# Top-k attention followed by an exact-GELU MLP: eleven odd items turned by VectorE and DRAM, with their product a slot later

## The chip, the cores and the metric

The kernel runs on one core of a Trainium2 chip. The metric is the device time of one execution in microseconds; the time before is the median of three runs. The engines are named as the profile names them: PE is TensorE (PEld its weight loads), DVE is VectorE, ACT is ScalarE, POOL is GpSimd, SP is SyncE, which issues nearly all DMAs.

## The reference

Attention over 8 batches, 8 heads, 576 positions and 64 columns per head, in which each row keeps its 32 largest scores; then an MLP with exact GELU on the 4608 x 512 result.

```python
scores = (1.0 / np.sqrt(D)) * np.matmul(q, k.transpose(0, 1, 3, 2))
kth = np.partition(scores, -32, axis=-1)[..., -32:-31]
scores = np.where(scores >= kth, scores, -1e9)
scores = scores - np.max(scores, axis=-1, keepdims=True)
attn = np.exp(scores)
attn = attn / (np.sum(attn, axis=-1, keepdims=True) + 1e-09)
x = np.matmul(attn, v)            # then (B, H, S, D) -> (B*S, H*D)
h = x @ w_in                      # 512 -> 2048
g = 0.5 * h * (1.0 + erf(h / sqrt(2)))
out = g @ w_out                   # 2048 -> 512
```

## The kernel before

**Items and slots.** Heads are taken in pairs; 576 rows are four tiles of 128 and a last 64. An item is one pair and one tile of rows; a "main" item has a tile of 128 rows of two heads, a "last" item the last 64 rows of four heads. There are 18 items per batch and 144 in all (`N`), and `RINGS` is 36, the number of items in two batches, after which the pattern repeats. One loop, `for n in range(ahead)`, records one slot after another; the program order on each engine is the order of these calls, since the schedule is written by hand. Tiles in pools make an instruction wait until the readers of the buffer's former contents are done.

**What an item goes through.** In slot n the loop records, for different items at once:

- `scores(n + 2)` on TensorE, into PSUM, and ScalarE's copies into the tile `s` (L408 and L416, last keys L373 and L381); in even slots two items' scores together;
- `top_k(n)` on VectorE: rounds of MAX8 and MATCH_REPLACE8 (L504, L507). Inside it stand `square_p(n - 2)` (L599) and, at its end, the reciprocal of item n - 1 (L525). GpSimd makes the lists (L468, L476), the threshold (L518, L519), the small addend (L531) and the normalisation (L573);
- `select` and `softmax` of item n - 1 on ScalarE (L538 and L550, with a load of the function's table);
- the turning of P of item n - 2, so that keys lie on partitions. There are two ways. By TensorE: one transpose for the last keys into bank `tp_t` (L651) and eight for the rest (L665), each followed by a copy of ScalarE into `pt` (L654, L680). Or "squared": VectorE turns blocks of 32 x 32 (L599), `write_p` writes the tile to DRAM in four DMAs (`turned<-s`, L609) and `read_p`, a slot later, reads it back into `pt` in four (`pt<-turned`, L619);
- `attend`, the product of `pt` with v for an even item and the odd one after it together (o, L736; for last rows L747), and ScalarE's copy of it into `xT` (L741, L757), which is recorded in `copies` and made by `copy_x`;
- pieces of the MLP, by `mlp(n)`: `h_ps` (L805), `seven` (L959, the seventh product of a Strassen-like block, copied by ScalarE at L977 or L980), and six more products in three groups of two (`y_ps`, L961), with ScalarE's gelus (L821) in odd slots. In some blocks the second matmul is plain (L923, L926), without `seven`.

Before the change an even main item is squared (except those at 12 modulo 36) and an odd one is turned by TensorE; their joint product for odd item i stands at the start of slot i + 3. For most last items `delayed` holds: their product comes later, in `mid`, behind `seven`, and `mids()` attends, copies `xT` and issues the next `read_p`. The loads of the next v stand in `soon` and are issued there as well.

**Buffers that set the order.** From slot 21 on (`few`), the small products `seven`, `o`, `t_ps`/`tp_t` all take the single PSUM bank with the tag `z`. `pt` is a single buffer. `s` has seven. SP works through its queue in order, and an issue that has to wait holds those behind it.

**ScalarE's order in odd slots.** For most odd slots (`ahead_of_x`) the two selects of item n - 1 come first, then the table and the gelus, the copy of `seven`, the table, and the two exponentials. In the odd slots from 15 to 23 modulo 36 the gelus and the copy of `seven` come first.

**Names that the change touches.** `squared` says which items go by VectorE and DRAM; `mid` is the list of products that this slot makes late; `bare(n)` moves two pieces of the MLP from one slot into the next; `room` is the number of pieces left for the place; `ODD` is 2.

Of the kernel before, what the change touches and what calls it, by code (L numbers as in the profile page):

```python
# [14 lines left out]
def kernel(  # L15
# [76 lines left out]
    def raw_of(n, pair):  # L92
        if n != "v":
            return raws[n][pair % 2 if pair < SQUARES else 0]
        return raws[n][pair % len(raws[n])]
# [7 lines left out]
    def issue(f):  # L103

        if held[0]:
            late_issues.append(f)
        else:
            f()
# [148 lines left out]
    items, starts = [], []  # L257
# [8 lines left out]
    def place_of(b, row):  # L266

        if row < SM:
            return b // 2 * RING + b % 2 * (SM + 2 * TL) + row
        return b // 2 * RING + SM + b % 2 * TL + row - SM  # L270

    N = len(items)
# [7 lines left out]
    def bank(name):  # L280

        tag = "z" if few[0] else ("z", "y0", "y1", "y2")[turn[0] % 4]
        turn[0] += 1
        return ps.tile([P, 512], f32, tag=tag, bufs=1, name=name)
# [68 lines left out]
    def row(i, e):  # L353
        return S_of[i][:, e * S : (e + 1) * S]
# [5 lines left out]
    def half(r, e):  # L360


        return slice((r ^ e) * TL, ((r ^ e) + 1) * TL)
# [169 lines left out]
    def select(i, e):  # L533

        if i < 0 or i >= N:
            return
        st, s = stat_of[i], row(i, e)
        nc.scalar.activation(s, s, func=AF.Prelu, bias=st["neg"][:, e : e + 1], scale=1.0, alpha=STEEP)  # L538
        selected.add((i, e))
# [3 lines left out]
    def softmax(i, e):  # L543

        if i < 0 or i >= N:
            return
        st, s = stat_of[i], row(i, e)
        if (i, e) not in selected:
            select(i, e)
        nc.scalar.activation(  # L550
            s, s, func=AF.Exp, bias=st["bias"][:, e : e + 1], scale=1.0,
            accum_out=st["den"][:, e : e + 1],
        )
# [23 lines left out]
    def squared(i):  # L577

        if not SINGLE.stop - 2 < i < N - 2:
            return False  # L580
        if items[i][1] == NM:
            return i % RINGS != RINGS // 2 - 1
        return i % 2 == 0 and i % RINGS != 12

    def delayed(i):

        return squared(i) and items[i][1] == NM
# [4 lines left out]
    RINGS = 2 * len(items) // B  # L592
# [18 lines left out]
    def read_p(i):  # L611

        if squared(i):
            d = turned.pop(i)
            if i % 2 == 0:
                pt_now[0] = pt_tile()
            cols = slice(i % 2 * P, (i % 2 + 1) * P)
            for k in range(P // SQ):
                nc.sync.dma_start(  # L619
                    out=pt_now[0][k * SQ : (k + 1) * SQ, :, cols], in_=d[:, :, k, :]  # L620
                )
# [77 lines left out]
    def copy_x():  # L699
        while copies:  # L700
            copies.pop()()
# [7 lines left out]
    def column(tok):  # L709

        at = tok % RING
        return at if at < COLS else at - COLS

    def attend(i):

        if i < 0 or i >= N:
            return False
        pair, t = items[i]
        b, at = divmod(pair, NP)
        if t < NM and t % 2 == 0:  # L720
            return False
        pt = pt_now[0]
        both = t == NM and delayed(i - 1) and not delayed(i)
        alone = t < NM or not delayed(i) or delayed(i ^ 1)
        o = shared.pop() if both else bank("o")
        off = 2 * TL if both else 0
        n, row = (2 * P, (t - 1) * P) if t < NM else (TL, SM)
        tok = place_of(b, row)
        gap = RING if t == NM else COLS if tok % RING >= COLS else RING - COLS
        assert read[0] >= tok - gap + n  # L730
        c = slice(column(tok), column(tok) + n)
        if t < NM:
            vt = raw_of("v", pair)
            for j in range(NJ):
                for e in range(2):
                    nc.tensor.matmul(  # L736
                        o[e * D : (e + 1) * D, 0:n], lhsT=vt[:, j, e, :],
                        rhs=pt[:, e * NJ + j if j < NM else NM, :],
                        start=(j == 0), stop=(j == NJ - 1),
                    )  # L740
            copies.append(lambda: nc.scalar.copy(out=xT[:, at, c], in_=o[:, 0:n]))  # L741
        else:
            for r in range(2):
                vt = raw_of("v", pair + r)
                for j in range(NJ):
                    for e in range(2):
                        nc.tensor.matmul(  # L747
                            o[e * D : (e + 1) * D, off + r * TL : off + (r + 1) * TL],
                            lhsT=vt[:, j, e, :],
                            rhs=pt[:, e * NJ + j if j < NM else NM, i % 2 * P :][:, half(r, e)],  # L750
                            start=(j == 0), stop=(j == NJ - 1),
                        )
            if not alone:
                shared.append(o)
            else:
                first = 0 if both else at
                copies.append(lambda: nc.scalar.copy(  # L757
                    out=xT[:, first : at + 2, c],
                    in_=o[:, 0 : off + 2 * TL].rearrange("p (r n) -> p r n", n=TL),
                ))  # L760

        if t == (NM if b % 2 == 0 else NM - 1):
            for r in range(2 if t == NM else 1):
                f = lambda r=r: load("v", pair + r + NP)
                if delayed(i):
                    soon.insert(0, f)
                elif both and r:
                    later.append(f)
                else:
                    issue(f)  # L770
        if at == (NP - 1 if t < NM else NP - 2):
            assert n_tok[0] == tok
            n_tok[0] = tok + n
        return True
# [285 lines left out]
    ODD = 2  # L1060
# [21 lines left out]
    def run_gelus():  # L1082
        while waiting:
            gelus(waiting.pop(0))
            if eager[0]:
                run_small(9)

    def run_small(room):

        while summing:  # L1090
            sums(summing.pop(0))
            room -= 4
        while small and room > 0:
            n, f = small.pop(0)
            f()
            room -= n
# [11 lines left out]
    def mlp(n):  # L1108
        for _ in range(n):
            if done[0] >= len(pieces) or pieces[done[0]][0] > ready[0] or left[0] == 0:  # L1110
                return
            pieces[done[0]][1]()
            done[0] += 1
            left[0] -= 1
            if eager[0]:
                run_gelus()
                run_small(9)
# [3 lines left out]

    def bare(n):

        return n - 4 in starts and delayed(n - 4)

    def room_in(n):

# [50 lines left out]
    for pair in range(2, n_pairs):  # L1178
        b, p = divmod(pair, NP)
        if pair >= SQUARES:  # L1180
            trio = transpose_qk(pair)
            for at, c in second[p] if b == 1 else squares_of[b % 2 * NP + p]:
                squares_in.setdefault(starts[b] + at, []).append(trio[c])
            continue
        for at, piece in zip(first.get(pair, slots_of[b % 2][p]), transpose_qk(pair)):
            prep_in.setdefault(starts[b] + at, []).append(lambda _, piece=piece: piece())
    sums_in = {START + 8 + j: j for j in range(FT // 2)}
    ahead = N + 4
    for n in range(ahead):

        held[0] = n < N and squared(n - 2)
        mid = [i for i in (n - 5, n - 4) if delayed(i) and n % 2 and (i % 2 or i in starts)]
        def stores_later(m):
            return m % 2 == 0 and delayed(m - 3) and m - 4 in starts

# [6 lines left out]
        def mids():  # L1202
            attend(mid.pop(0))
            if not mid:
                copy_x()
                read_p(n - 3)
                issue_soon()
        few[0] = n > START + 2
        ahead_of_x = few[0] and n > RINGS // 2 and (n % 2 == 0 or not -4 < n % RINGS - RINGS // 2 < 6)
# [19 lines left out]
        if even_last:  # L1229
            product = attend(n - 4)  # L1230
            attend(n - 3)
            issue_soon()
        else:
            product = not delayed(n - 3) and attend(n - 3)
        if len(mid) == 2:
            mids()
        late = n > START
# [35 lines left out]
        if n != 1 and not late:  # L1273
            softmax(n - 1, 1)
        if few[0]:
            if n % 2 or not ahead_of_x:
                softmax(n - 1, 0)
            if n % 2:
                if ahead_of_x:
                    softmax(n - 1, 1)  # L1280
                mlp(ODD)
                if mid:
                    mids()
        mlp(1)
        prep = prep_in.pop(n, [])
        if n == 0:
# [105 lines left out]
```

## Time and profile before

| | us |
|---|---|
| median of three runs | 1472.87 (1472.58 to 1473.02) |
| the profiled execution | 1472.55 |
| its span | 1470.8 |
| ScalarE busy | 1070.4 |
| GpSimd busy | 1137.7 |

The TensorE clock was full in all 40 slices. In the rows of the timeline the first number is the start within the span, the second the duration, and what stands in brackets at the end is the idle time of the engine just before with what ended it. A float32 matmul shows as two records. Matmuls overlap in the records, so the time of a group on TensorE is read from the start of one row to the start of the next. A group's row gives busy time in all and the mean in ns.

### The profile page before, as it was taken

Reading aid. Unit: us, or ns where it says so; the run is one execution under the profiler, and the core shown is the slowest. Engines: PE = TensorE matmul, PEld = TensorE weight load, DVE = VectorE, ACT = ScalarE, POOL = GpSimd, SP = SyncE. Lnnn points to the kernel's source line nnn. Section 1 sums busy time; section 2 is a strip of 40 time slices with the busy share of each in tenths; the row PEclk is TensorE's granted clock in tenths of the full one; section 3 lists DMA queues with packets and bytes.
Section 4 is the critical chain, followed back from the end, with each engine's and each line's share of the span. In section 5 each row is a group of like instructions: output and inputs, shape, how many; then the busy total and the mean of one; then the engine's idle time right before and its main releaser. Section 6 shows DMA issues by size and latency. Waiting matters only on the chain. (4 is left out here: it accounts for less than half of the span.)

```text
span 1470.8 us, 26630 instructions
## 1 busy us (share of the span) xinstructions
PE 1451.4 (99%) x8720; PEld 1135.5 (77%) x8720; DVE 1312.2 (89%) x3328; ACT 1070.4 (73%) x1905; POOL 1137.7 (77%) x1290
## 2 busy tenths in 40 slices
PE   8999999999999999999999999999999999999999
PEld 6776677877777777887777778787777778787887
DVE  7999899999999899999999999999989989999701
ACT  7999977777777786767777777776777767687620
POOL 6877667878798878877798978887888887887632
PEclk9999999999999999999999999999999999999999
DMA  7425310045435246355534345344543423533200
GB/s 198 146 87 127 81 48 1 24 93 107 83 72 97 56 85 132 65 102 106 105 76 82 71 71 119 84 93 96 102 99 74 89 51 78 127 67 76 59 15 15
DMA packets 527050, 123.51 MB, mean 84 GB/s; under 512 B 452256, under 2 KB 518464, under 8 KB 526912
## 3 DMA queue, kind: packets, MB, share of 16 engines
q1 hardware_dynamic: 525648, 121.39, 38.6%
q8 instruction: 69, 1.13, 0.3%
q14 instruction: 69, 0.57, 0.1%
q10 hardware_dynamic: 1200, 0.39, 0.1%
q0 software_dynamic: 64, 0.03, 0.0%
HBM read 78.70 MB, written 43.06 MB: 83 GB/s over the span
## 5 line engine op out<-in xcount | busy, mean ns | idle before, releaser
L805 PE MATMUL h_ps<-xT,w_in_sb 128*128 128x256 f32 (+1 forms) x2560 | 534.1, 361 | 0.0
L805 PEld LDWEIGHTS h_ps<-xT,w_in_sb 128*128 128x128 f32 x2560 | 437.5, 190 | 73.3 <-issue 12.9
L504 DVE MAX8 top<-lists 128x8 f32<-128x576 f32 (+1 forms) x792 | 475.1, 638 | 0.0
L507 DVE MATCH_REPLACE8 lists<-top,lists 128x288 f32<-128x288 f32 (+1 forms) x528 | 307.2, 587 | 0.0
L538 ACT ACTIVATE s<-s,stat 128x576 f32<-128x576 f32 x288 | 218.1, 781 | 106.5 <-POOL stat L518 106.4
L573 POOL TENSOR_TENSOR s<-s,stat 128x1152 f32<-128x1152 f32 x135 | 285.9, 2118 | 0.3 <-DVE stat L525 0.3
L550 ACT ACTIVATE s<-s,stat 128x576 f32<-128x576 f32 x288 | 224.2, 782 | 7.3
L468 POOL TENSOR_TENSOR lists<-s 128x576 int32<-128x576 int32 x133 | 189.8, 1427 | 0.0
L476 POOL TENSOR_TENSOR lists<-lists 128x576 int32<-128x576 int32 x132 | 186.0, 1409 | 4.0
L531 POOL TENSOR_SCALAR stat<-stat 128x2 f32<-128x2 f32 x144 | 31.4, 218 | 167.1 <-ACT s L550 157.4
L416 ACT ACTIVATE s<-s_ps 128x1024 f32<-128x1024 f32 x127 | 125.3, 1033 | 41.3 <-PE s_ps L408 41.2
L736 PE MATMUL o<-pt,raw_v 128*64 128x256 f32 x1280 | 152.9, 384 | 1.5 <-ACT pt L680 0.5
L736 PEld LDWEIGHTS o<-pt,raw_v 128*64 128x64 f32 x1280 | 87.5, 136 | 85.8 <-issue 40.9
L961 PE MATMUL y_ps<-w_out_sb,sum 128*128 128x256 f32 x472 | 140.4, 379 | 0.0
L408 PE MATMUL s_ps<-kt,qm 64*128 64x512 f32 x512 | 129.6, 619 | 0.8 <-ACT s L414 0.8
L821 ACT ACTIVATE g<-h_ps 128x512 f32<-128x512 f32 x144 | 78.2, 594 | 69.7 <-PE h_ps L805 68.9
L507 DVE MATCH_REPLACE8 lists<-first,lists 128x288 f32<-128x288 f32 x264 | 114.0, 437 | 0.0
L961 PE MATMUL y_ps<-w_out_sb,g 128*128 128x256 f32 x480 | 113.4, 379 | 0.0
L443 DVE TENSOR_TENSOR lists<-s 128x576 f32<-128x576 f32 x133 | 108.8, 818 | 4.2 <-ACT s L381 2.1
L504 DVE MAX8 first<-lists 128x8 f32<-128x288 f32 x268 | 106.3, 435 | 0.0
L680 ACT COPY pt<-tp 128x1024 f32<-128x1024 f32 x76 | 77.6, 1021 | 39.0 <-PE tp L665 38.9
L961 PEld LDWEIGHTS y_ps<-w_out_sb,g 128*128 128x128 f32 x480 | 91.2, 190 | 12.4
(162 smaller groups left out, 2408.9 us busy)
## 6 DMA issues: line engine op xcount, KB each, us to landing
turned<-s SPq DMA_DIRECT2D x228, 144.0 KB, 3.5
pt<-turned SPq DMA_DIRECT2D x228, 144.0 KB, 3.2
raw_v<-in_v_dram SPq DMA_DIRECT2D x64, 128.0 KB, 2.7
raw_q<-in_q_dram SPq DMA_DIRECT2D x112, 72.0 KB, 2.4
raw_k<-in_k_dram SPq DMA_DIRECT2D x112, 72.0 KB, 2.4
out_dram<-y SPq DMA_DIRECT2D x30, 256.0 KB, 2.2
w_out_sb<-in_moe_w_in_dram SPq DMA_DIRECT2D x14, 511.8 KB, 4.8
w_out_sb<-in_moe_w_out_dram SPq DMA_DIRECT2D x10, 511.8 KB, 4.1
```

Of the source, the lines that this page charges most:

```text
L408: nc.tensor.matmul(s_ps[:, e], lhsT=q_t[rows, :], rhs=kt[rows, main_keys(pair)], start=True, stop=True)
L416: nc.scalar.activation(spread(s, S + TL, SM), s_ps, func=AF.Copy, scale=scale)
L468: nc.gpsimd.tensor_tensor(t[:, :, 1].bitcast(i32), a.bitcast(i32), b.bitcast(i32), op=ALU.add)
L476: nc.gpsimd.tensor_tensor(into_of(i)[:, :, 1].bitcast(i32), both, top, op=ALU.subtract)
L504: nc.vector.max(x[:, e], src[:, e])
L507: nc.vector.match_replace(dst[:, e], x[:, e], src[:, e], LOWEST)
L538: nc.scalar.activation(s, s, func=AF.Prelu, bias=st["neg"][:, e : e + 1], scale=1.0, alpha=STEEP)
L550: nc.scalar.activation(s, s, func=AF.Exp, bias=st["bias"][:, e : e + 1], scale=1.0, accum_out=st["den"][:, e : e + 1],)
L573: nc.gpsimd.tensor_tensor(s, s, wide, op=ALU.mult)
L736: nc.tensor.matmul(o[e * D : (e + 1) * D, 0:n], lhsT=vt[:, j, e, :], rhs=pt[:, e * NJ + j if j < NM else NM, :], start=(j == 0), stop=(j = ...
L805: nc.tensor.matmul(h_tile(u)[:, i, :], lhsT=w_in_sb[:, ko, f * P : (f + 1) * P], rhs=xT[:, ko, c0 : c0 + n], start=(ko == 0), stop=(ko == ...
L961: nc.tensor.matmul(acc[names][:, k], lhsT=lhsT, rhs=rhs, start=(j == 0 and k == 0), stop=(j == FT // 2 - 1 and k == 1),)
```

## The change

Eleven odd main items (at 3, 13, 25 and 31 modulo 36, from item 36 to item 135) are squared too: items 39, 49, 61, 67, 75, 85, 97, 103, 111, 121 and 133. Their square stands in VectorE's slot i + 2, the write behind it, the read at the start of slot i + 3; the product moves from the start of slot i + 3 into `mid` of slot i + 4, behind `seven` and one more piece of the MLP (in blocks without `seven`, behind the first two pieces), with the copy into `xT` between the two exponentials. The read of item i + 1 into `pt` follows that product. `bare` moves two pieces of the MLP from slot i + 2 into slot i + 3. In slots 59, 95 and 131 the second last-row product stands one piece earlier, and its copy into `xT` ahead of the first select.

```diff
         if items[i][1] == NM:
             return i % RINGS != RINGS // 2 - 1
-        return i % 2 == 0 and i % RINGS != 12
+        return moved(i) or (i % 2 == 0 and i % RINGS != 12)
+
+    LATER = (3, 13, 25, 31)
+
+    def moved(i):
+
+        return RINGS <= i < N - 8 and i % RINGS in LATER
...
-                if delayed(i):
+                if delayed(i) or moved(i):
                     soon.insert(0, f)
...
-        return n - 4 in starts and delayed(n - 4)
+        return moved(n - 3) or (n - 4 in starts and delayed(n - 4))
...
+    starts_next = [x + 1 for x in starts]
...
         mid = [i for i in (n - 5, n - 4) if delayed(i) and n % 2 and (i % 2 or i in starts)]
+        if moved(n - 4):
+            mid = [n - 4]
...
-            product = not delayed(n - 3) and attend(n - 3)
+            product = not delayed(n - 3) and not moved(n - 3) and attend(n - 3)
...
         if few[0]:
+            room = ODD if n % 2 else 0
+            if mid and mid[0] in starts_next:
+                mlp(1)
+                mids()
+                room -= 1
             if n % 2 or not ahead_of_x:
                 softmax(n - 1, 0)
-            if n % 2:
-                if ahead_of_x:
-                    softmax(n - 1, 1)
-                mlp(ODD)
-                if mid:
-                    mids()
+            if mid:
+                mlp(1)
+                mids()
+                room -= 1
+            if n % 2 and ahead_of_x:
+                softmax(n - 1, 1)
+            mlp(room)
         mlp(1)
```

## The prediction

> **What bounds the kernel now.** I read the busy times first, then the groups by form, the waits, and the timelines of the slots that the change touches.
>
> ```profile
> span 1470.8 us, 26630 instructions
> PE 1451.4 (99%) x8720; PEld 1135.5 (77%) x8720; DVE 1312.2 (89%) x3328; ACT 1070.4 (73%) x1905; POOL 1137.7 (77%) x1290
> ...
> DVE stat L525 <- POOL stat L531: 74.8, 74, 6.2
> ```
>
> TensorE has work for 1451.4 of 1470.8 us: time leaves the kernel when its matmuls leave, and grows by every wait put in front of it. VectorE is next at 89%, so both are close to the limit and one slot (one item of the loop) decides by its own chain. Now the groups whose number changes, and slot 43, the first that gets a moved product:
>
> ```profile
> L599 DVE STREAM_TRANSPOSE s<-s 128x1152 f32<-128x1152 f32 x57 | 77.6, 1362 | 0.0
> L665 PE MATMUL tp<-ident,s 128*128 128x128 f32 x624 | 81.0, 273 | 0.0
> ...
> 406.54 1.04 PE L665 MATMUL tp<-ident,s 128*128 128x128 f32 x8
> 407.42 0.60 PE L961 MATMUL y_ps<-w_sum,g 128*128 128x256 f32 x2
> ...
> 411.16 2.38 PE L736 MATMUL o<-pt,raw_v 128*64 128x256 f32 x20
> 413.46 2.86 PE L805 MATMUL h_ps<-xT,w_in_sb 128*128 128x256 f32 x12
> ...
> 420.70 1.03 PE L959 MATMUL seven<-w_sum,g 128*128 128x256 f32 x4
> 421.56 1.89 PE L961 MATMUL y_ps<-w_out_sb,g 128*128 128x256 f32 x8
> 423.29 0.59 PE L961 MATMUL y_ps<-w_sum,sum 128*128 128x256 f32 x2
> ...
> 424.74 0.49 PE L373 MATMUL tp_t<-kt,qm 128*128 128x128 f32 x2 [0.43 <-ACT p L980]
> ...
> 428.74 1.56 PE L408 MATMUL s_ps<-kt,qm 64*128 64x512 f32 x6
> ```
>
> ```profile
> 420.59 1.44 ACT L538 ACTIVATE s<-s,stat 128x576 f32<-128x576 f32 x2 [3.73 <-POOL stat L518]
> ...
> 423.34 1.08 ACT L821 ACTIVATE g<-h_ps 128x512 f32<-128x512 f32 x2
> 424.31 0.38 ACT L980 COPY p<-seven 128x256 f32<-128x256 f32 x1
> ...
> 410.90 0.17 DVE L525 RECIPROCAL stat<-stat 128x2 f32<-128x2 f32 x1 [2.17 <-POOL stat L531]
> ...
> 420.17 0.14 DVE L525 RECIPROCAL stat<-stat 128x2 f32<-128x2 f32 x1
> ```
>
> The chain to see: VectorE ends the top-k of item 42 at 420.17; GpSimd makes its threshold; ScalarE, idle 3.73 us for it, runs the two selects at 420.59, then the gelus, then copies `seven` out of PSUM until 424.69. Every small product of the late slots (`seven`, `o`, the last keys) shares the one PSUM bank `z`. Already today TensorE waits 0.43 us there before it may write `tp_t`.
>
> **The change, part by part.**
>
> *Transposes removed.* Eight take 407.42 - 406.54 = 0.88 us; with the ninth, for the last keys, 0.99 us for each of the 11 items, at most 10.9 us. ScalarE loses the two copies that followed; it waits in these slots, so I count nothing for that.
>
> *Product moved.* The 20 records of `o` take 413.46 - 411.16 = 2.30 us. They now stand behind `seven` and one piece (four records, half of the eight that take 423.29 - 421.56 = 1.73 us). That is the costly step: `o` needs bank `z`, which holds `seven` until ScalarE has copied it. Four kinds of slot follow; numbers are of the first of each, since the 36-slot pattern repeats.
>
> *Kind A, offset 3 (slots 43, 79, 115).* The old order reaches the point behind the first piece at 421.56 + 0.86 = 422.42. Without transposes and earlier product that is 422.42 - 0.99 - 2.30 = 419.13. The copy of `seven` still ends at 424.69, because the VectorE chain before it does not get shorter (its own reciprocal at 410.90 waits for a GpSimd queue, and the added 1.36 us square of this item fits into the 2.17 us idle there). So TensorE waits about 5 us. `o` then runs to 427.0, eight records (1.73 us) follow, and `tp_t` starts at 428.7 in place of 424.74: 4.0 us later. What is late next is the scores, at 428.74, and through them the selects of the next slot; TensorE is busy 99% of the span and has no idle time to give the 4.0 back, so it stays. Three times: +12.0.
>
> *Kind B, offset 13 (slots 53, 89, 125).*
>
> ```profile
> 516.04 1.09 PE L423 MATMUL s_ps<-kt 64*64 64x512 f32 x8
> 518.89 1.89 PE L961 MATMUL y_ps<-w_out_sb,g 128*128 128x256 f32 x8
> ...
> 517.20 1.02 ACT L427 ACTIVATE s<-s_ps 128x1024 f32<-128x1024 f32 x1 [4.41 <-PE s_ps L423]
> 520.50 0.38 ACT L980 COPY p<-seven 128x256 f32<-128x256 f32 x1
> ```
>
> Here gelus come ahead of the selects, and ScalarE waits for TensorE's own scores, so the copy moves with TensorE. From the scores the copy ends after 520.88 - 516.04 = 4.84 us, and `o` is reached after 518.89 + 0.86 - 516.04 = 3.71: a wait of 1.13 against 0.99 saved. Three times +0.14: +0.4.
>
> *Kind C, offset 25 (slots 65, 101, 137).*
>
> ```profile
> 619.90 0.14 DVE L525 RECIPROCAL stat<-stat 128x2 f32<-128x2 f32 x1
> 630.42 0.17 DVE L525 RECIPROCAL stat<-stat 128x2 f32<-128x2 f32 x1 [1.05 <-POOL stat L531]
> ...
> 620.07 0.22 POOL L518 TENSOR_SCALAR stat<-top 128x2 f32<-128x2 f32 x1 [0.53 <-DVE stat L525]
> 630.17 0.22 POOL L531 TENSOR_SCALAR stat<-stat 128x2 f32<-128x2 f32 x1
> ...
> 636.63 0.18 ACT L550 ACTIVATION_READ_ACCUMULATOR s<-s,stat 128x1 f32 x1
> 636.81 0.39 PE L373 MATMUL tp_t<-kt,qm 128*128 128x128 f32 x2
> ```
>
> The square is put ahead of 619.90, where VectorE does not wait: 1.36 us later. GpSimd starts behind that reciprocal and works on to 630.17, so 630.42 moves by 1.36 too and its 1.05 us idle covers nothing. This slot has no `seven`; but the copy of `o` now stands behind the first exponential, and `tp_t` needs the bank that it frees. That exponential ends at 636.81 + 1.36 = 638.2, the copy about 0.25 later: 638.4 for `tp_t` against 636.81, +1.6, the saved transposes lost in the wait. Three times: +4.8.
>
> *Kind D, offset 31 (slots 71, 107).*
>
> ```profile
> 688.37 0.14 DVE L525 RECIPROCAL stat<-stat 128x2 f32<-128x2 f32 x1
> 692.67 0.38 ACT L980 COPY p<-seven 128x256 f32<-128x256 f32 x1
> 694.96 0.38 PE L373 MATMUL tp_t<-kt,qm 128*128 128x128 f32 x2
> ```
>
> As kind A, with VectorE late twice by then (2 x 1.36 = 2.7): the copy of `seven` ends at 693.05 + 2.7 = 695.7; 2.30 + 1.73 puts `tp_t` at 699.7, 4.8 behind, of which 1.6 was there from kind C. So +3.2, twice: +6.4.
>
> *Last-row copy moved up (slots 59, 95, 131).*
>
> ```profile
> 575.83 1.39 PE L747 MATMUL o<-pt,raw_v 128*64 128x64 f32 x40
> 579.28 0.49 PE L373 MATMUL tp_t<-kt,qm 128*128 128x128 f32 x2 [1.00 <-ACT xT L757]
> ...
> 574.88 0.38 ACT L980 COPY p<-seven 128x256 f32<-128x256 f32 x1
> 578.99 0.24 ACT L757 COPY xT<-o 128x128 f32<-128x128 f32 x1
> ```
>
> The copy at 578.99 leaves its place behind an exponential, and the 1.00 us wait goes. The product, one piece (0.86) earlier, would arrive at 574.97 and waits until 575.26, about 0.3. So -0.7, three times: -2.2 (bounds -3.0 and 0).
>
> *DMAs.* 88 more on SP's queue. The read of the next P shares the single `pt` tile, so SP waits for the moved product with it.
>
> ```profile
> 422.39 2.54 SPq L619 DMA_DIRECT2D pt<-turned  x4
> ...
> pt<-turned SPq DMA_DIRECT2D x228, 144.0 KB, 3.2
> ```
>
> Four issues and the last landing are about 5.2 us. From the end of the moved product to the next one lie 1.73, then 428.74 - 424.74 = 4.0, then 1.9 of scores, 7.6 us: covered with 2.4 to spare. Loads queued behind it have a slot or more. I count zero; a read slowed by 3 us would cost 0.6 each, 7 in all.
>
> *The array's clock.* The new waits of 4 to 5 us are longer than any that this trace shows in its middle.
>
> ```profile
> 1.04 4.21 PE L1148 MATMUL warm<-raw_v 128*128 128x128 f32 x18 [1.04 <-DVE raw_v L85]
> ...
> 6.10 0.71 PE L307 MATMUL tp_qk<-ident,raw_q 128*128 128x128 f32 x5
> ```
>
> After the start's idle time 18 records take 4.21 us, 0.23 each; later ones take 0.14 or less. A cold spell like that costs some 2 us. Behind the 1.00 us wait at 579.28 nothing slows, so the price of each of the five long waits (A and D) lies between 0 and 2, 10 us in all; measured waits in the middle show 0, and I take 0 in the sum and 10 for the range. The Trainium skill, page "TensorE: Matmul & The Clock Gate", Part 1, says that the array falls to half clock after one idle window of some 3.4 us and needs about as long a busy one to recover. By that rule some or all of the five waits would end cold; no trace here shows it yet.
>
> **Sum.** 12.0 + 0.4 + 4.8 + 6.4 - 2.2 = +21.4 us. The profiled execution took 1472.55 (its span 1470.8 and 1.75 around it); the median of the runs is 1472.87. That gives 1494.0 for the first and **1494.3** for the median.
>
> **Rivals.**
>
> *The array goes cold in the long waits.* Same mechanism, plus up to 10: 1504.3. For it: the start rows. Against it: the waits here are at the edge of what could do it. That rule of the skill is this rival.
>
> *Faster: the bank is free in time.* If ScalarE's copy of `seven` came 5 us earlier in kinds A and D, by a top-k that ends earlier, nothing would wait and the removed matmuls decide: -10.9 - 2.2 = -13.1, 1459.8. For it: TensorE is at 99%. Against it: the 3.73 us that ScalarE idles in front of the selects is VectorE's, not TensorE's, and VectorE gets work added. It decides from the point where the copy ends before 419.1.
>
> *VectorE alone.* The bank wait is hidden and only VectorE's squares in kinds C and D count: 5 x 1.36 = 6.8, less 2.2: 1477.5. For it: no idle time at 619.90 and 688.37. Against it: the same lateness reaches bank `z`.
>
> *No change.* Waits and savings cancel (1470 to 1476); kind B alone does that.
>
> **How the numbers follow.** Forecast 0.58 (its own range 1487 to 1502: A between 3 and 5 us, the last-row bounds, the DMA's 7), cold array 0.22, VectorE alone 0.05, no change 0.03, faster 0.12. About 0.2%, 3 us, is what a measurement of this kernel can tell from no change. So faster 0.12, same 0.03, slower 0.85. The range goes from 1483, where half of the 21 us is hidden, to 1507, the cold case with the DMA's share of it; VectorE alone, no change and faster stay outside, 0.20 together.
>
> **What would show it.** In the changed profile `o` should have idle time in front of it released by the copy of `seven`, some 5 us in slots 43, 79, 115, 4 in 71 and 107, 1 in 53, 89, 125; `tp_t` should wait 2 us for the copy of `o` in 65, 101, 137; the 1.00 in 59, 95, 131 should be gone; `L665` should count 536, `L599` 68. A TensorE clock below full in the slices after the waits would show the cold array. I am wrong if the copy of `seven` is seen ending before `o` is reached, or if idle time on VectorE absorbs the squares at offsets 25 and 31.

## The result, and the profile after

| | before | after |
|---|---|---|
| median, us | 1472.75 (1472.58 to 1473.02, 4 runs) | 1504.16 (1503.81 to 1504.61, 4 runs) |
| profiled execution, its span, us | 1472.55, 1470.8 | 1503.81, 1502.0 |
| TensorE's granted clock over the span | 1.000 | 0.992 |

The ratio is 1.0213 (95%: 1.0200 to 1.0226): the change costs 31.4 us. The forecast was 1494.3, in a range from 1483 to 1507. The granted clock is the share of its full rate at which the profile shows TensorE clocked.

The head of the page of after, and two rows of its groups (count, then total and mean of one, then idle time in front and its releasers):

```profile
span 1502.0 us, 26598 instructions
PE 1452.0 (97%) x8621; PEld 1128.8 (75%) x8621; DVE 1332.2 (89%) x3339; ACT 1059.2 (71%) x1883; POOL 1138.1 (76%) x1290
```

```profile
L742 PE MATMUL o<-pt,raw_v 128*64 128x256 f32 x1280 | 161.7, 400 | 30.8 <-ACT p L986 27.1 <-DMA pt<-turned 3.0 <-ACT pt L676 0.4
L671 PE MATMUL tp<-ident,s 128*128 128x128 f32 x536 | 69.6, 273 | 0.0
L605 DVE STREAM_TRANSPOSE s<-s 128x1152 f32<-128x1152 f32 x68 | 92.7, 1363 | 0.0
```

Lines of the changed kernel stand six higher than those of before in this part of the code: `o` is L742, the copy of `seven` L986, the transposes L671, VectorE's squares L605. Transposes went from 624 to 536 and squares from 57 to 68, as written. The transposes took 11.4 us of matmuls away (81.0 to 69.6), yet TensorE's busy time rose from 1451.4 to 1452.0: other matmuls became slower. And its share fell from 99 to 97%: it now waits. The waits of TensorE say for whom (total, number, longest):

```profile
PE o L742 <- ACT p L986: 27.1, 8, 5.3
PE tp_t L373 <- ACT xT L747: 5.0, 3, 2.1
...
PE o L742 <- DMA pt<-turned: 3.0, 3, 1.4
```

Eight waits for the copy of `seven` are the eight moved products of kinds A, B and D; three of `tp_t` for the copy of `o` are kind C. One of kind A, on TensorE and then on ScalarE:

```profile
418.51 1.03 PE L967 MATMUL y_ps<-w_out_sb,g 128*128 128x256 f32 x4
424.82 4.06 PE L742 MATMUL o<-pt,raw_v 128*64 128x256 f32 x20 [5.29 <-ACT p L986]
428.82 1.13 PE L967 MATMUL y_ps<-w_out_sb,g 128*128 128x256 f32 x4
430.65 0.38 PE L373 MATMUL tp_t<-kt,qm 128*128 128x128 f32 x2
```

```profile
420.67 1.44 ACT L538 ACTIVATE s<-s,stat 128x576 f32<-128x576 f32 x2 [5.94 <-POOL stat L518]
423.42 1.08 ACT L827 ACTIVATE g<-h_ps 128x512 f32<-128x512 f32 x2
424.39 0.38 ACT L986 COPY p<-seven 128x256 f32<-128x256 f32 x1
```

The first fence carries two costs. TensorE stands still for 5.29 us, until the copy of `seven` at 424.39 has left bank `z`. Then the 20 records of `o` take 4.06 us, where 2.38 was their time before. The second cost is in the windows of this kernel (stretch, its length, busy time and count of PE, PEld, DVE, ACT, POOL, then the granted clock, the DMA share and GB/s):

```profile
419.00:424.80 5.80, 0.53 (x3) 0.13 (x1) 5.76 (x18) 4.09 (x7) 5.07 (x7) 1.00 0.48 75
424.80:428.30 3.50, 3.48 (x18) 2.01 (x20) 3.50 (x8) 2.14 (x3) 1.36 (x1) 0.51 0.00 0
428.30:432.00 3.70, 3.70 (x23) 2.96 (x20) 0.84 (x3) 1.62 (x5) 1.77 (x4) 1.00 0.33 96
...
1002.10:1005.60 3.50, 3.50 (x22) 3.19 (x23) 3.46 (x9) 2.06 (x5) 1.88 (x5) 1.00 0.83 249
```

The array works at half clock for the 3.5 us behind the wait, and at full clock again from 428.3. All five long waits (A and D) end like this; the 2.10 us wait of kind C at 1002.09, last row, does not. The other four `o` behind a long wait:

```profile
701.33 4.05 PE L742 MATMUL o<-pt,raw_v 128*64 128x256 f32 x20 [4.11 <-ACT p L986]
...
782.95 4.20 PE L742 MATMUL o<-pt,raw_v 128*64 128x256 f32 x20 [5.29 <-ACT p L986]
...
1059.59 4.07 PE L742 MATMUL o<-pt,raw_v 128*64 128x256 f32 x20 [4.11 <-ACT p L986]
...
1141.22 4.26 PE L742 MATMUL o<-pt,raw_v 128*64 128x256 f32 x20 [5.28 <-ACT p L986]
```

Against 2.38 the five are 1.68 + 1.67 + 1.82 + 1.69 + 1.88 = 8.7 us longer. So the theory for the experiments: some 22.7 us (net of the transposes saved) are the waits in bank `z`, behind ScalarE's copy, which stands behind selects that wait for VectorE's top-k; some 8.7 us are the clock that falls in the five longest of them. The rivals: that VectorE's 11 squares (11 x 1.36 = 15.0 us) or the single `pt` tile set the loss, and that the slower `o` has another cause than the clock.

### The profile page after: what moved, and what is told of

Its sections match the earlier page's. It is cut to its first block, busy times and chain, and to the rows that moved or that the text cites. A ratio compares the mean times of both kernels' runs of the same rounds, so it can differ in the third digit from the quotient of the medians.

```text
span 1502.0 us, 26598 instructions
## 1 busy us (share of the span) xinstructions
PE 1452.0 (97%) x8621; PEld 1128.8 (75%) x8621; DVE 1332.2 (89%) x3339; ACT 1059.2 (71%) x1883; POOL 1138.1 (76%) x1290
## 5 line engine op out<-in xcount | busy, mean ns | idle before, releaser
L811 PEld LDWEIGHTS h_ps<-xT,w_in_sb 128*128 128x128 f32 x2560 | 438.4, 190 | 69.6 <-issue 11.3
L742 PE MATMUL o<-pt,raw_v 128*64 128x256 f32 x1280 | 161.7, 400 | 30.8 <-ACT p L986 27.1
L742 PEld LDWEIGHTS o<-pt,raw_v 128*64 128x64 f32 x1280 | 91.6, 143 | 115.3 <-issue 41.2
L531 POOL TENSOR_SCALAR stat<-stat 128x2 f32<-128x2 f32 x144 | 31.3, 218 | 191.4 <-ACT s L550 185.4
L443 DVE TENSOR_TENSOR lists<-s 128x576 f32<-128x576 f32 x133 | 114.4, 861 | 9.4 <-ACT s L381 7.2
L967 PEld LDWEIGHTS y_ps<-w_out_sb,sum 128*128 128x128 f32 x472 | 89.7, 190 | 12.2
```

The source lines that it names most:

```text
L742: nc.tensor.matmul(o[e * D : (e + 1) * D, 0:n], lhsT=vt[:, j, e, :], rhs=pt[:, e * NJ + j if j < NM else NM, :], start=(j == 0), stop=(j = ...
L811: nc.tensor.matmul(h_tile(u)[:, i, :], lhsT=w_in_sb[:, ko, f * P : (f + 1) * P], rhs=xT[:, ko, c0 : c0 + n], start=(ko == 0), stop=(ko == ...
L967: nc.tensor.matmul(acc[names][:, k], lhsT=lhsT, rhs=rhs, start=(j == 0 and k == 0), stop=(j == FT // 2 - 1 and k == 1),)
```

## The experiments

All are edits of the changed kernel. Gains and losses are taken against the median of before beside the same runs (1473.18 for the first four, 1473.25 for the others).

**No moved products at all: the copy of the last rows alone.**

```diff
-    LATER = (3, 13, 25, 31)
+    LATER = ()
```

> LATER is empty: no item is moved, only the last-row product and its copy stand earlier in slots 59, 95 and 131. The prediction's step: the 1.00 us wait of tp_t goes and nothing takes its place, -2.2 us against the kernel before (1470.6). Rival, from the changed kernel's timeline (o in slot 60 waits 1.29, 0.38 and 1.36 us for pt<-turned): the time is handed on to the read of the next P, which in the kernel before landed just ahead of its product, so -0.6 to 0 us (1472.2 to 1472.8), with a wait of PE o for DMA pt<-turned in slots 60, 96, 132.

Measured: 1472.22 us (1470.87 to 1473.02), ratio 0.9993 (0.9984 to 1.0002). The wait of 1.00 is gone, but not the time. This kernel's rows of TensorE in slots 59 and 60, then of SP's queue:

```profile
575.91 1.39 PE L753 MATMUL o<-pt,raw_v 128*64 128x64 f32 x40 [0.27 <-ACT p L986]
...
579.05 0.38 PE L373 MATMUL tp_t<-kt,qm 128*128 128x128 f32 x2
...
583.15 1.99 PE L408 MATMUL s_ps<-kt,qm 64*128 64x512 f32 x8
586.01 2.38 PE L742 MATMUL o<-pt,raw_v 128*64 128x256 f32 x20 [0.88 <-DMA pt<-turned]
```

```profile
573.40 4.87 SPq L615 DMA_DIRECT2D turned<-s  x4
580.84 2.54 SPq L625 DMA_DIRECT2D pt<-turned  x4
```

The same queue and the same product before the change:

```profile
572.65 4.57 SPq L609 DMA_DIRECT2D turned<-s  x4
579.96 2.54 SPq L619 DMA_DIRECT2D pt<-turned  x4
```

```profile
583.28 1.99 PE L408 MATMUL s_ps<-kt,qm 64*128 64x512 f32 x8
585.20 2.38 PE L736 MATMUL o<-pt,raw_v 128*64 128x256 f32 x20
```

`tp_t` no longer waits, and the last-row product waits 0.27, as forecast. But the next product stands still 0.88 us for its P; before, it came with no idle time at all. The starts of the two kernels cannot be compared as they are: this kernel was already 0.60 us late when the slot's `seven` began (573.75 against 573.15), and as late at its first `o` (44.75 against 44.14). Counted from `seven`, TensorE reaches the scores 0.73 us earlier than before (583.15 - 573.75 = 9.40 against 583.28 - 573.15 = 10.13), and the read leaves 0.28 us later (7.09 against 6.81). So most of the wait is the time that TensorE has just won, and the smaller part is the later read. Why that is later was not followed further. The result is what the rival in the expectation had named.

**The long waits filled with other matmuls.** Identity times identity into a PSUM tile that nothing reads, ahead of the moved product of kinds A and D.

```diff
+    FILL = {7: 22, 35: 16}
...
+            if moved(n - 4) and n % RINGS in FILL:
+                filler = pair_tile("filler")
+                for _ in range(FILL[n % RINGS]):
+                    nc.tensor.matmul(filler[:, 0, 0:P], lhsT=ident, rhs=ident, start=True, stop=True)
```

> The changed kernel with idle matmuls of ident by ident put ahead of the moved product at offsets 3 (22 matmuls) and 31 (16), into a PSUM tile that nobody reads: the wait for the bank stays, but the array does not stand still. If the array's clock is what adds to the waits (23.9 us at half rate in the changed kernel's profile, 11.9 us lost), the time falls by 10 to 12 us, to about 1492 to 1494, the clock is full in every slice and the moved product takes 2.3 us in place of 4.06. Rival: the clock reading is a by-product and the product is slow for another reason (operands, the pt tile just landed): the time stays at 1504.

Measured: 1495.84 us (1494.80 to 1497.45), ratio 1.0156 (1.0142 to 1.0170), mean clock 1.000. Its slot 43:

```profile
419.00 1.03 PE L967 MATMUL y_ps<-w_out_sb,g 128*128 128x256 f32 x4
419.86 5.07 PE L1216 MATMUL filler<-ident 128*128 128x128 f32 x44
425.31 2.38 PE L742 MATMUL o<-pt,raw_v 128*64 128x256 f32 x20 [0.37 <-ACT p L986]
```

`o` takes 2.38 again. It starts 6.31 us behind the piece in front of it (425.31 - 419.00), as in the changed kernel (424.82 - 418.51), so the other matmuls do not delay it. Doing useless work in the wait makes the kernel faster. The loss falls from 31.4 to 22.7 us: the clock was worth 8.7 us, the sum of the five longer `o` above. What remains is the waits themselves. The gain is smaller than the 10 to 12 us expected, because that figure took all 23.9 us at half clock for work; in slots 79 and 115 the half clock began some 3 us before `o` did, and without these 6 us half of the rest is 8.9.

**The copy of `seven` ahead of the selects, in the four kinds of slot.** The gelus and the copy no longer stand behind VectorE's top-k on ScalarE; VectorE, SP and `pt` keep their work. Kind B's slots had this order already, and those of kind C have no `seven`, only the gelus.

```diff
+        ahead_of_x = ahead_of_x and not moved(n - 4)
```

> The changed kernel with one change: in the eleven slots with a moved product the selects stand behind the gelus and the copy of seven, as they already do at offset 13, so that bank z is given back without waiting for VectorE. If the bank held behind VectorE's top-k is the cause, the waits of o of 5.3 and 4.1 us shrink to about 1 us or nothing, no half clock is left, and the time is 1471 to 1478 (the second exponential then stands behind the copy of pt, which may cost about 1 us per slot). Rival: VectorE's eleven squares (15.0 us) or the single pt tile are the cause: the time stays above 1485.

Measured: 1477.98 us (1477.74 to 1479.02), ratio 1.0035 (1.0021 to 1.0049), clock 1.000. ScalarE and TensorE in slot 43 of this kernel:

```profile
419.28 0.37 ACT L986 COPY p<-seven 128x256 f32<-128x256 f32 x1
421.23 0.78 ACT L538 ACTIVATE s<-s,stat 128x576 f32<-128x576 f32 x1 [1.58 <-POOL stat L518]
```

```profile
419.08 1.03 PE L967 MATMUL y_ps<-w_out_sb,g 128*128 128x256 f32 x4
420.03 2.38 PE L742 MATMUL o<-pt,raw_v 128*64 128x256 f32 x20
```

The copy comes 5.1 us earlier (419.28 for 424.39), although this kernel reached the piece in front of `o` 0.57 us later (419.08 against 418.51), and `o` follows at 420.03 without a wait. One line of order takes 26.6 of the 31.4 us away, the 8.7 of the clock among them. The 15.0 us of squares and the single `pt` are still there, so they did not set the loss. The 4.8 us that remain are not their whole price, though: they are what is left after the saving of up to 10.9 us of transposes. Several short waits are left, the largest group on the read of P:

```profile
PE o L742 <- DMA pt<-turned: 6.3, 5, 2.0
...
PE o L742 <- ACT p L986: 3.0, 3, 1.0
PE tp_t L373 <- ACT p L986: 2.4, 5, 0.8
```

**Each kind alone.** Four kernels with one kind each and the copy of the last rows; since that copy alone gave -1.0, each kind costs its difference plus 1.0, with the uncertainty of that figure (its interval is 0.3 us slower to 2.4 us faster) in each.

```diff
-    LATER = (3, 13, 25, 31)
+    LATER = (13,)
```

(and likewise `(3,)`, `(25,)`, `(31,)`)

> LATER is (13,): only items 49, 85 and 121 are moved, where the gelus already stand ahead of the selects. The prediction's kind B: a wait of 1.0 to 1.13 us for the bank against 0.99 us of transposes saved, three times +0.14, so within 1 us of e1_last_only. Rival: the write, the read and the square cost here too, +2 us or more each, 6 us in all.

> LATER is (3,): items 39, 75 and 111 alone, kind A. Against e1_last_only (1472.2): three times 4.0 us by the prediction's step, and 4 to 6 us for the spells at half clock behind the three waits of 5.3 us (the changed kernel had one of 3.4 us and two of 6.8 us there): about 1488 to 1490. Rival, that a lateness of 4 us is given back later, where TensorE is less pressed: below 1480.

> LATER is (25,): items 61, 97 and 133 alone, kind C. By the prediction's step tp_t waits for the copy of o behind an exponential that VectorE's square has made 1.36 us later: three times 1.6 us, 1477.0, with full clock throughout. Rival: the saved transposes outweigh it, 1470 to 1472.

> LATER is (31,): items 67 and 103 alone, kind D without kind C ahead of it. VectorE is late once (1.36 us), the copy of seven ends at 694.2 by the rows of the kernel before, tp_t starts 3.3 us later: twice 3.3, and about 1.7 us of half clock each: 1479 to 1482. Rival, that VectorE's lateness is the whole of it: twice 1.36, 1475.

| kind alone | median, us | ratio (95%) | mean clock | cost of the kind | forecast |
|---|---|---|---|---|---|
| B, offset 13 | 1472.08 (1471.31 to 1474.01) | 0.9995 (0.9986 to 1.0004) | 1.000 | -0.1 | +0.4 |
| A, offset 3 | 1490.26 (1489.21 to 1491.35) | 1.0115 (1.0101 to 1.0129) | 0.994 | +18.0 | +12.0 |
| C, offset 25 | 1477.48 (1476.90 to 1480.34) | 1.0033 (1.0022 to 1.0044) | 0.999 | +5.2 | +4.8 |
| D, offset 31 | 1482.69 (1482.28 to 1483.22) | 1.0064 (1.0050 to 1.0078) | 0.996 | +10.4 | +6.4 |

The four costs make 33.5; all four together cost 31.4 + 1.0 = 32.4 over the kernel without any. They add up within the intervals, so no kind hides another to a degree that these runs can tell. A and D lie well above the forecast, and 0.3 and 0.7 us above the ranges expected for these two runs; both have a clock below full. The waits and what follows them, for A alone:

```profile
425.27 4.54 PE L742 MATMUL o<-pt,raw_v 128*64 128x256 f32 x20 [5.29 <-ACT p L986]
...
777.89 4.30 PE L742 MATMUL o<-pt,raw_v 128*64 128x256 f32 x20 [5.29 <-ACT p L986]
...
1129.92 4.06 PE L742 MATMUL o<-pt,raw_v 128*64 128x256 f32 x20 [5.29 <-ACT p L986]
```

```profile
425.30:430.30 5.00, 5.00 (x22) 2.67 (x23) 3.61 (x8) 2.54 (x5) 1.31 (x1) 0.51 0.00 0
777.90:781.50 3.60, 3.60 (x18) 2.09 (x20) 3.60 (x8) 2.11 (x3) 1.34 (x1) 0.50 0.00 0
1129.90:1132.70 2.80, 2.78 (x14) 1.66 (x16) 2.80 (x7) 2.13 (x3) 1.36 (x1) 0.51 0.00 0
...
781.30:782.10 0.80, 0.80 (x6) 0.24 (x2) 0.23 (x1) 0.00 (x0) 0.00 (x0) 0.68 0.00 0
1132.70:1133.50 0.80, 0.80 (x8) 0.42 (x6) 0.80 (x2) 0.00 (x0) 0.00 (x0) 0.57 0.07 20
```

and the stretches behind the two waits of D alone (4.11 us each):

```profile
695.00:698.70 3.70, 3.70 (x18) 2.08 (x15) 3.69 (x8) 2.27 (x5) 0.68 (x1) 0.56 0.01 1
1045.40:1050.20 4.80, 4.80 (x21) 2.52 (x22) 4.34 (x9) 2.33 (x4) 1.33 (x1) 0.50 0.08 12
```

Length times the missing share of the clock is what is lost. For A the first three stretches give 5.00 x 0.49 + 3.60 x 0.50 + 2.80 x 0.49 = 5.6 us; the last two rows show that the half clock went on to 781.8 and 1133.4, which adds 0.3 x 0.5 + 0.7 x 0.5 = 0.5, so 6.1. For D it is 3.70 x 0.44 + 4.80 x 0.50 = 4.0. Without it A costs about 11.9 and D 6.4; the loss is that of one profiled execution, taken from a median, so the tenths are an estimate. The first `o` of D alone (694.33) is the exception among the long waits: its first microsecond is at full clock, and the half clock begins at about 695.4.

The 0.999 of C belongs to the starting phase, some 70 us into the span, far from slot 65. The stretch in the profile of C alone:

```profile
68.00:72.00 4.00, 2.65 (x15) 2.22 (x14) 4.00 (x14) 4.00 (x6) 3.04 (x5) 0.72 0.56 213
```

Here the clock fell at about 69.9, behind an idle time of TensorE of only 1.35 us, and stayed half for some 3.4 us; the same wait in the kernel before, 1.33 us long, left it full. Of C's 5.2 us a part lies elsewhere, too: `tp_t` waits 1.06 us at 810.98, in slot 81, which has no moved product.

**A version from the parts that work: offsets 3 and 25, with the copy first.**

```diff
-    LATER = (3, 13, 25, 31)
+    LATER = (3, 25)
...
+        ahead_of_x = ahead_of_x and not moved(n - 4)
```

> LATER is (3, 25) with the selects behind the copy of seven in these six slots, as in e3_copy_first, whose trace shows waits of 0.2 to 0.3 us at offset 3, none at offset 25 and 1.4 to 2.0 at offset 31. If what is left of the 0.99 us saved per item reaches the end, 3 x 0.5 + 3 x 1.0 = 4.5 us below e1_last_only: 1468. Rival: VectorE, which gets the squares and a second exponential that stands behind the copy of pt, hands the gain back by a wait elsewhere: 1471 to 1474.

Measured: 1471.10 us (1470.55 to 1472.19), ratio 0.9987 (0.9978 to 0.9996). It is 2.2 us below before, where the transposes of its six items and the last rows' copy would have given 6 x 0.99 + 1.0 = 6.9 us. In slot 43 nothing waits in front of the product; the largest wait for data that is left in the middle is an old one:

```profile
419.76 2.38 PE L742 MATMUL o<-pt,raw_v 128*64 128x256 f32 x20
```

```profile
PE o L742 <- DMA pt<-turned: 3.2, 3, 1.7
```

These are the same three reads as with the last-row copy alone (3.3 us in all there), and what they cost is already in the 1.0 us of that copy, so they do not explain the 4.7 us that are missing. Where those went stays open. The time lies in the range of the expectation's rival, 1471 to 1474, and not at its 1468. It is the best kernel of this study, by little more than its interval.

## Why the prediction was right in its direction and 10 us short in its point

**Bank `z` behind ScalarE behind VectorE (kinds A and D): right, in mechanism and size.** The idle time in front of `o` is 5.29 and 4.11 where 5 and 4 were forecast, released by the copy of `seven` each time. `tp_t` of slot 43 starts at 430.65; less the 1.68 us of slower `o` that is 428.97, where 428.7 was forecast. Without the clock A costs about 11.9 (12.0 forecast) and D 6.4 (6.4). That the order on ScalarE is the cause, and not only the name that the profile gives to the wait, is shown by the copy put first, which removes the wait and 26.6 us.

**Kind B: right.** The waits are 1.01 each (1.13 forecast) and the kind alone costs nothing that can be told from zero.

**Kind C: right in its mechanism.** TensorE waits for the copy of `o` 1.03, 1.25 and 2.05 us in the kernel with C alone, and the kernel pays 5.2 us (4.8 forecast). That the two figures lie so close may be chance: the profiled run has the wait in slot 81 and the half clock of its starting phase, which the forecast did not know.

**The array's clock: the term that was mis-sized.** The step read "measured waits in the middle show 0, and I take 0 in the sum and 10 for the range". The runs put 8.7 there: 1.7 to 1.9 us for each of five waits, near the 2 us that had been read from the array's start. The mistake was the choice of the row. A wait of 1.00 us was taken to speak for waits of 4 and 5, though the trace of before had none of that length; the row that was set aside, the slow matmuls of the start, gave the right price. In nine of ten waits of 4.1 to 5.3 us (five in the changed kernel, three in A alone, two in D alone) the product behind the wait ran at half clock from its start, to within 0.2 us, and in the tenth the half clock came some 1 us later. The Trainium skill, "TensorE: Matmul & The Clock Gate", Part 1, has the array fall to half clock after an idle window of some 3.4 us. The trace agrees for waits of this length. The rival that was named after it is what happened. That its figure, 1504.3, meets the 1504.16 so closely is luck: its clock term was 1.3 us too high (10 for 8.7) and its last-row term 1.2 us too low (-2.2 for -1.0). The point of 1494.3, and the narrower range of 1487 to 1502 that went with it, missed.

**The copy of the last rows: wrong in size.** The step was -2.2 us; alone it gave -1.0, with an interval that reaches to no change. Its mechanism held (the 1.00 is gone, 0.27 comes before the last-row product), but the step did not ask what TensorE would meet next, having won that time: the read of P.

**The DMAs at zero: right for the moved products as they stand in the changed kernel, wrong beside the last rows.** No moved product waits for a read there, but the product behind the last rows does (0.88, 0.69 and 1.74 us with that copy alone, where before only the third had waited, 0.49). The count of 2.4 us to spare was made in slot 43 alone, and there it holds. It does not hold for every kind once the wait for the bank is gone: with the copy first, a moved product of kind D (1041.92) waits 1.97 us for its read.

**The sum, mended.** 12.0 + 0.4 + 4.8 + 6.4 - 1.0 = 22.6 for the waits, 22.7 measured where the clock stays full; with 8.7 for the clock 31.3, against 31.4. The terms of the four kinds here are the forecast ones.

## What to carry to other kernels

Before an instruction is moved past another one that uses the same PSUM bank, follow the release of that bank back over every engine: here it ended at VectorE's top-k, two engines away, and the position of one copy on ScalarE decided 26.6 of 31.4 us. Price a wait of TensorE for the clock as well: in the middle of these kernels a wait of up to 2.1 us cost itself, and one of 4.1 us or more cost 1.6 to 2.5 us on top; no wait between the two was measured, and in the starting phase a wait of 1.35 us was once followed by half clock. A wait taken out of an in-order engine is a gain only up to the next thing that it waits for, so look at the operand of the next instruction as well.

## What had not been expected of the hardware

The clock can fall inside the wait, well before the waiting matmul starts. Slot 79 of the changed kernel, where TensorE is idle from 777.66 (782.95 - 5.29):

```profile
777.70:779.80 2.10, 0.00 (x0) 0.00 (x0) 2.06 (x6) 1.01 (x2) 1.48 (x4) 1.00 0.93 145
779.90:782.90 3.00, 0.00 (x0) 0.00 (x0) 3.00 (x12) 2.97 (x5) 2.92 (x3) 0.50 0.03 6
782.95:786.60 3.65, 3.65 (x18) 2.13 (x20) 3.63 (x8) 2.11 (x3) 1.34 (x1) 0.50 0.00 0
786.70:790.10 3.40, 3.40 (x19) 2.67 (x16) 0.52 (x2) 1.62 (x5) 1.60 (x4) 1.00 0.29 87
```

Here the clock is full for the first 2.1 us of the wait and half from 779.9 on, some 2.2 us after the last matmul; it stays half for 3.65 us of work. In slot 43 it fell only as the wait ended. So the half clock lasted about 3.4 us in the one and 6.8 us in the other, with nearly the same loss of work, 1.7 and 1.8 us. The Trainium skill, "TensorE: Matmul & The Clock Gate", Part 1, has the clock fall after an idle window of some 3.4 us. In slot 79 some 2.2 us of idle time were enough, and in the starting phase of C alone 1.35 us with a shorter wait of 0.31 us some 1.5 us earlier; what the window was counted from no run shows. Kind A alone makes the spread plain: three waits of the same 5.29 us were followed by 5.0, 3.9 and 3.4 us of work at half clock.

Left open: where the 4.7 us of the last version went, why the clock fell once behind a wait of 1.35 us and elsewhere not, and why the read behind the last rows leaves later. A second bank for `o`, which would remove the wait without a new order on ScalarE, was not tried, and neither was a read of P that starts earlier behind the last rows.
